# A masked attention and MLP kernel on Trainium2: the second MLP product of chunks 4 to 11 in seven block products per pair

## The chip, the cores and the metric

The kernel runs on one core of one Trainium2 chip. The metric is the device time of one execution in microseconds (us); three runs of the kernel before gave a median of 678.27 us (676.78 to 681.28). The engines are TensorE (PE; its weight loads are listed apart as PEld), VectorE (DVE), ScalarE (ACT), GpSimd (POOL) and SyncE (SP, which here only issues DMA transfers).

## The reference, cut to what matters

```python
# attention: batch 4, 8 heads, 768 positions, 64 per head, float32
scores = q @ k.T / sqrt(64)      # kept where key < 4 (sinks) or 0 <= query - key < 128
x = softmax(scores) @ v          # brought to 3072 tokens x 512
# MLP
h = x @ w_in                                            # 512 -> 2048
g = np.maximum(h, 0.0) + alpha * np.minimum(h, 0.0)     # alpha: one per column of h
out = g @ w_out                                         # 2048 -> 512
```

## The kernel before

**Tiling.** The 3072 tokens are cut into 12 chunks (`NCHUNK`) of 256 (`QC`), three per batch. The 2048 columns of h are 16 blocks (`NF`) of 128, called f. For a chunk c and a block f, GEMM1 (`gemm1`, L887) computes a transposed block of h, 128 x 256, in a PSUM bank, and GEMM2 (`gemm2`, L906) adds the product of that block of g with 128 rows of w_out to two PSUM banks of 128 tokens x 512, which hold the sums over all 16 f. The work on PE is done in a 32-bit form (`F32R`) that holds fewer bits of the mantissa; each operand is split into a high and a low part, and a product is three matmuls: high x high, high x low, low x high. So GEMM1 has 4 x 3 = 12 matmuls of 256 columns per (c, f) (L894), and GEMM2 has 2 x 3 = 6 of 512 columns (L931, L932 and L929).

**From GEMM1 to GEMM2.** ACT scales the PSUM bank by alpha (L898), DVE takes the maximum of the bank and that (L899), which is g; ACT casts g to its high part gh (L900), DVE subtracts for the low part gl (L901). gh and gl have three buffers each, g two. When a chunk is complete, ACT copies both banks (L937) and SP issues two output transfers of 256 KB (L938). For the last f of the last chunk, lines L912 to L923 do this bank by bank, with the transfers issued from ACT.

**Attention of the next chunk** is woven into GEMM1 and GEMM2 of the present one. Per head: SP loads q and k (`stage`, L443), ACT casts (L561, L562) and DVE subtracts (L563 for k, L565 for q) to make the parts, PE makes scores for two halves u (L597, L598), DVE masks and takes the minimum (L610), ACT takes the exponential (L614), DVE scales (L655), GpSimd makes the small sink products (L659). For every pair of heads DVE transposes blocks of 32 (L741), SP sends them through a DRAM scratch and back (L744, L746), and DVE applies triangle masks (L757, L759, L770). At the end `av_four` (L848) multiplies by v on PE (L786, L859, L875), and ACT and DVE write the high and the low part of x, `xh` and `xl` (L881, L882), which have two buffers, so that one chunk's x can be written while another's is read.

**Weights** are loaded and converted once, in chunks 0 and 1, into 16 resident tiles `fin` (high and low parts of both matrices).

**The order of work** is written out by a planner. Every piece of work is an `op` with an engine, a cost and the values that it reads and writes; `draw` (L153) plays all engines forward by these costs and picks, at each step, the operation that can start first, with ties within 0.1 to 0.2 us broken by rank. A PE operation's rank is its place in the program; any other has the rank of the first operation that needs it, or of its own place plus 12 (`LATEST`). Some operations name a second engine (`other`), and the planner takes the one that starts first, with 0.3 us against the second. The result is a fixed order for each engine; SP's DMA issues are ordered by it too. An `op` can be marked `locks`: the planner then lets no two marked operations on DVE and GpSimd overlap. In the kernel before nothing is marked. The loop at L1065 lays out (c, f) in order, GEMM2 two blocks behind GEMM1 (`LAG`).

**PSUM** has eight banks: two for scores (`s`), two for attention products (`pa`), two for h, two for the output sums (`o`).

## Time and profile before

| | us |
|---|---|
| median of three runs | 678.27 (676.78 to 681.28) |
| profiled execution, first to last instruction (its span; the time around it is not recorded) | 676.2 |
| PE busy | 663.8 |
| DVE busy | 525.8 |
| ACT busy | 397.5 |
| GpSimd busy | 34.5 |
| output copies of chunks 2, 3, 10 and 11 (start) | 209.43, 262.23, 628.72, 669.94 |

A period between two output copies holds one chunk's GEMM1 and GEMM2 and the attention of the next. DMA moves 85.19 MB at a mean of 126 GB/s over the span. In the timeline, "0.39 PE L931 MATMUL" is an instruction of 0.39 us of line 931; matmuls overlap, so their pace is the distance of their starts. An arrow in brackets names what ended the idle time before an instruction. In a group's row the numbers after the bar are the busy time of the group, the mean ns of one and the idle time of the engine in front of them.

### The profile page before, as it was taken

The page shows a single profiled execution, that of the slowest core. Times are in us where ns is not written, and L with a number is a line of the kernel's source. Part 1 is how long each engine was busy: PE and PEld are TensorE (multiplying, and loading weights), DVE is VectorE, ACT ScalarE, POOL GpSimd, SP SyncE. Part 2 cuts the span into 40 slices and gives each one's busy share as a digit, 9 for nine tenths or more (in the row PEclk, how much of TensorE's full clock was granted, in tenths as well). Part 3 has the DMA queues.
Part 4 walks back from the last instruction along what each step waited for, and adds up shares of the span by engine and source line. Part 5 has one row for each costly group of instructions (what it writes and reads, how often), then busy time and mean ns, then how long its engine had stood idle before and what let it go on. Part 6 is the DMA issues. An engine that isn't in the chain of part 4 may idle for free.

```text
span 676.2 us, 13243 instructions
## 1 busy us (share of the span) xinstructions
PE 663.8 (98%) x4532; PEld 580.5 (86%) x4534; DVE 525.8 (78%) x1750; ACT 397.5 (59%) x1066; POOL 34.5 (5%) x115
## 2 busy tenths in 40 slices
...
GB/s 314 229 277 151 241 187 39 127 71 147 122 133 107 122 148 93 145 132 95 141 118 114 143 107 93 163 140 61 172 128 78 161 128 88 142 94 17 32 2 35
DMA packets 58683, 85.19 MB, mean 126 GB/s; under 512 B 9072, under 2 KB 35056, under 8 KB 58608
## 3 DMA queue, kind: packets, MB, share of 16 engines
...
q8 instruction: 37, 0.61, 0.4%
...
## 4 chain that ended last, share of the span: by engine, by line
PE 83%; DVE 9%; ACT 5%; issue 2%; POOL 0%; DMA 0%; ACTq 0%; SPq 0%; POOLq 0%
PE bank L894 35%; PE bank L931 12%; PE bank L932 11%; PE bank L929 11%; PE bank L786 3%; PE bank L598 3%; PE bank L597 3%; PE bank L875 2%; DVE wa L396 2%; ACT pt L614 1%; ACT wa L382 1%; DVE wa L394 1%; DVE w L404 1%; DVE g L899 1%; DVE gl L901 1%
## 5 line engine op out<-in xcount | busy, mean ns | idle before, releaser
L894 PE MATMUL bank<-xh,w 128*128 128x256 f32 x1536 | 307.9, 283 | 0.4 <-DVE g L899 0.2
L894 PEld LDWEIGHTS bank<-xh,w 128*128 128x128 f32 x1536 | 250.6, 189 | 9.0 <-DVE g L899 3.0
L894 PE MATMUL bank<-xl,w 128*128 128x256 f32 x768 | 215.1, 280 | 0.1
L898 ACT ACTIVATE g<-bank,param 128x256 f32<-128x256 f32 x192 | 90.5, 472 | 117.4 <-PE bank L894 113.1
L931 PE MATMUL bank<-w,gh 128*128 128x512 f32 x382 | 151.7, 397 | 0.2 <-ACT gh L900 0.2
L932 PE MATMUL bank<-w,gh 128*128 128x512 f32 x382 | 150.1, 393 | 0.0
L894 PEld LDWEIGHTS bank<-xl,w 128*128 128x128 f32 x768 | 145.2, 189 | 4.4 <-DVE xl L808 0.3
L614 ACT ACTIVATE pt<-pt,nm 128x260 f32<-128x260 f32 (+1 forms) x192 | 94.5, 493 | 53.5 <-DVE nm L610 53.1
L899 DVE TENSOR_TENSOR g<-bank,g 128x256 f32<-128x256 f32 x192 | 79.7, 419 | 51.4 <-ACT g L898 50.9
L929 PE MATMUL bank<-w,gl 128*128 128x512 f32 x382 | 119.5, 394 | 0.0
L900 ACT CAST gh<-g 128x256 fp32r<-128x256 f32 x192 | 76.9, 404 | 59.7 <-DVE g L899 59.6
L901 DVE TENSOR_TENSOR gl<-g,gh 128x256 fp32r<-128x256 f32 x192 | 80.5, 423 | 26.5 <-ACT gh L900 23.0
L610 DVE CUSTOM_DVE_ANT_0 pt<-bank,masks 128x260 f32<-128x260 f32 (+1 forms) x192 | 75.0, 401 | 19.3 <-PE bank L598 15.5
L929 PEld LDWEIGHTS bank<-w,gl 128*128 128x128 f32 x382 | 70.7, 188 | 16.2 <-issue 0.7
L931 PEld LDWEIGHTS bank<-w,gh 128*128 128x128 f32 x382 | 71.9, 188 | 9.5 <-ACT gh L900 0.7
L932 PEld LDWEIGHTS bank<-w,gh 128*128 128x128 f32 x382 | 71.9, 188 | 8.3
L563 DVE TENSOR_TENSOR kq<-stage,kq 64x392 fp32r<-64x392 f32 x80 | 45.3, 566 | 2.7
L659 POOL TENSOR_TENSOR sink<-pt,ri 128x8 f32<-128x8 f32 x80 | 20.8, 264 | 504.7 <-DVE ri L644 358.8
L597 PE MATMUL bank<-kq 128*128 128x260 f32 (+1 forms) x160 | 44.4, 278 | 1.3 <-DVE nm L610 1.3
L598 PE MATMUL bank<-kq 128*128 128x260 f32 (+1 forms) x160 | 45.0, 281 | 0.0
L655 DVE CUSTOM_DVE_ANT_0 comb<-pt,ri 128x128 f32<-128x128 f32 x136 | 43.1, 343 | 0.4
L561 ACT CAST kq<-stage 128x392 fp32r<-128x392 f32 x80 | 40.9, 512 | 0.7 <-ACT pt L614 0.2
...
## 6 DMA issues: line engine op xcount, KB each, us to landing
...
swap<-comb SPq DMA_DIRECT2D x36, 256.0 KB, 2.0
comb<-swap SPq DMA_DIRECT2D x36, 256.0 KB, 3.2
...
out_dram<-ob SPq DMA_DIRECT2D x22, 256.0 KB, 3.5
...
```

What stands on the lines that cost most here:

```text
L597: nc.tensor.matmul(s[:, w0], qh()[:, qs], ks()[:, kw], start=True, stop=False)
L598: nc.tensor.matmul(s[:, w0], ql()[:, qs], ks()[:, kw], start=False, stop=True)
L610: op("DVE", dve(n), lambda: nc.vector.tensor_tensor_reduce(out=pt.at[:, u, w0], in0=s.at[:, w0], in1=masks[:, i, w0], scale=-0.125, scalar ...
L614: op("ACT", exp(n), lambda: nc.scalar.activation(pt.at[:, u, w0], pt.at[:, u, w0], AF.Exp, bias=nm.at[:, h, u:u + 1], scale=-1.0, accum_ou ...
L894: nc.tensor.matmul(h(), fin.at[:, 0, part, ks], rhs.at[:, kt], start=(kt == 0 and n == 0), stop=(kt == KT - 1 and n == 2))
L898: op("ACT", act(QC, True), lambda: nc.scalar.activation(g.at, h(), AF.Copy, scale=alt[:, f:f + 1]), reads=[bk, known("param")], writes=[g])
L899: op("DVE", dve(QC), lambda: nc.vector.tensor_tensor(g.at, h(), g.at, ALU.max), reads=[bk], writes=[g])
L900: op("ACT", cast(QC), lambda: nc.scalar.copy(gh.at, g.at), reads=[g], writes=[gh])
L901: op("DVE", dve(QC), lambda: nc.vector.tensor_tensor(gl.at, g.at, gh.at.bitcast(F32), ALU.subtract), reads=[g, gh], writes=[gl])
L929: nc.tensor.matmul(o2[j].at, gl.at[:, js], fin.at[:, 1, 0], start=False, stop=(f == NF - 1))
L931: nc.tensor.matmul(o2[j].at, gh.at[:, js], fin.at[:, 1, 0], start=(f == 0), stop=False)
L932: nc.tensor.matmul(o2[j].at, gh.at[:, js], fin.at[:, 1, 1], start=False, stop=False)
```

## The change

From chunk 4 (`SECOND`) on, GEMM2 takes two f blocks at a time. Their two 128 x 256 blocks of g and the two 128 x 512 row blocks of w_out are seen as 2 x 2 blocks (g in blocks of 128 tokens, w_out in halves of 256 columns, `HALF`), and the product is made with seven block products instead of eight (`seven`), each of three matmuls of 256 columns. For it:

- `blocks` makes the sums of g blocks: per pair one sum of 256 and two of 128 elements, on GpSimd or, where the planner finds that earlier, on DVE. The high and low parts are made of 2 + 2 + 3 blocks of 128 instead of 4, in new tiles ta, tb and ha (two buffers), hb and hc (one).
- `prepare` makes the combined weights in chunk 2, per pair p with eight GpSimd operations and two ACT casts, and writes them to a DRAM scratch `tees`. `exchange` loads one combined block over half a resident weight tile; the three others are loaded again for each chunk and pair, in three transfers of 256 KB into four buffers `st`. These are the former second buffers of xh and xl, which have one from chunk 4 on.
- The products go into four PSUM banks (`o` twice, `z`, `y`) and are combined at the end of a chunk by one ACT copy and five DVE operations, then sent out in two transfers (from ACT in the last chunk).
- The four banks s and pa become z, y, one bank `s2` for scores and one `pa2`; `av_four` uses pa2 and s2.
- From the attention of chunk 5 on, q's low part goes to GpSimd, or to DVE where that is earlier. These, the sums, the new low parts and `prepare` are marked `locks`.
- The attention of the next chunk is spread over 13 of 16 blocks (`SOON`) with `av_four` at the last, and some operations get earlier due times (`DUE`). GEMM2 of a pair comes one pair behind its GEMM1. `after_all` makes the new uses of a shared tile wait for all former users.

The diff, cut to its core:

```diff
+SECOND = 4
+SOON = 13
+DUE = {'bank': 4, 'scores': 5, 'swap': 8, None: 14}
+HALF = DM // 2
...
+    both = pool.tile([P, 4, HALF], F32, name="both")
+    plan.kind("ob", [both[:, 2 * i:2 * i + 2].rearrange("p b x -> p (b x)") for i in range(2)])
+    plan.kind("ob2", [both])
+    xs = {n: [pool.tile([P, KT, QC], F32R, name=f"{n}{i}") for i in range(2)] for n in ("xh", "xl")}
+    for n in xs:
+        plan.kind(n, xs[n])
+        plan.kind(n + "2", xs[n][:1])
+    plan.kind("st", [xs[n][1][:, 2 * i:2 * i + 2] for n in xs for i in range(2)])
+    exact = pool.tile([P, 16 * P], F32, name="exact")
+    cut = pool.tile([P, 18 * P], F32R, name="cut")
+    plan.kind("g", [exact[:, i * P:(i + 2) * P] for i in (12, 14)])
+    plan.kind("gh", [cut[:, i * P:(i + 2) * P] for i in (6, 8, 10)])
+    plan.kind("gl", [cut[:, i * P:(i + 2) * P] for i in (12, 14, 16)])
+    plan.kind("prep", [exact[:, :12 * P]])
+    some_blocks = lambda t, a, n: t[:, a * P:(a + n) * P].rearrange("p (b x) -> p b x", x=P)
+    plan.kind("ta", [some_blocks(exact, i, 3) for i in (0, 13)])
+    plan.kind("tb", [some_blocks(exact, i, 5) for i in (3, 8)])
+    plan.kind("ha", [some_blocks(cut, i, 4) for i in (0, 4)])
+    plan.kind("hb", [some_blocks(cut, 8, 4)])
+    plan.kind("hc", [some_blocks(cut, 12, 6)])
+    for name, i in (("s2", 0), ("z", 1), ("pa2", 2), ("y", 3)):
+        plan.kind(name, [banks[i]])
+    tees = [held(scratch.tile([P, 4, 2, HALF], F32, name=f"tee{i}")) for i in range(NF // 2)]
...
-           reads=[st, (kq, "q")], writes=[(kq, "l")])
+        low = lambda on: on.tensor_tensor(ql(), q_raw(), qh().bitcast(F32), ALU.subtract)
+        if c > SECOND:
+            op("POOL", pool2(QC), lambda: low(nc.gpsimd), reads=[st, (kq, "q")], writes=[(kq, "l")], locks=True,
+               other=("DVE", dve(QC), lambda: low(nc.vector)))
+        else:
+            op("DVE", dve(QC), lambda: low(nc.vector), reads=[st, (kq, "q")], writes=[(kq, "l")])
         prep[c, h] = (kq, qh, ql, ks)
 
...
         else:
             pair = (h,)
-            banks_ = [val("s")]
+            banks_ = [val("s2" if c > SECOND else "s")]
+            if c == SECOND + 1 and h == u == 0:
+                late.append((banks_[0], ("s", "pa")))
...
     def begin_x(c, p):
         if p == 0:
-            xh[c], xl[c] = val("xh"), val("xl")
+            xh[c], xl[c] = (val("xh2"), val("xl2")) if c >= SECOND else (val("xh"), val("xl"))
+            if c == SECOND:
...
         def some(kt):
@@ -894,6 +937,8 @@
                 nc.tensor.matmul(h(), fin.at[:, 0, part, ks], rhs.at[:, kt], start=(kt == 0 and n == 0), stop=(kt == KT - 1 and n == 2))
         for kt in range(KT):
             op("PE", 3 * mm(QC), lambda kt=kt: some(kt), reads=[fin, (x1, kt), (x2, kt)], writes=[bk], tail=R_TAIL)
+        if c >= SECOND:
+            return blocks(c, f, bk)
         g, gh, gl = val("g"), val("gh"), val("gl")
         op("ACT", act(QC, True), lambda: nc.scalar.activation(g.at, h(), AF.Copy, scale=alt[:, f:f + 1]), reads=[bk, known("param")], writes=[g])
+    def blocks(c, f, bk):
+
+        if f % 2 == 0:
+            twos[c, f // 2] = [val(n) for n in ("ta", "tb", "ha", "hb", "hc")]
+        ta, tb, ha, hb, hc = five = twos[c, f // 2]
+        h = lambda: bk.at[:, :QC].rearrange("p (b x) -> p b x", x=P)
+
+        def either(cost, cost2, run, reads, writes):
+            op("POOL", cost, lambda: run(nc.gpsimd), reads=reads, writes=writes, locks=True, other=("DVE", cost2, lambda: run(nc.vector)))
+
+        def cast_part(to, t, a, n):
+            op("ACT", cast(n * P), lambda: nc.scalar.copy(to.at[:, :n], t.at[:, a:a + n]), reads=[(t, i) for i in range(a, a + n)], writes=[(to, 0)])
+
+        def low_part(to, t, a, n):
+            op("DVE", dve(n * P), lambda: nc.vector.tensor_tensor(to.at[:, n:], t.at[:, a:a + n], to.at[:, :n].bitcast(F32), ALU.subtract),
+               reads=[(to, 0)] + [(t, i) for i in range(a, a + n)], writes=[(to, 1)], locks=True)
+        t, steps_ = ((ta, slice(0, 3, 2)), (tb, slice(3, 5)))[f % 2]
+        place, keys = lambda: t.at[:, steps_], [(t, i) for i in range(5)[steps_]]
+        op("ACT", act(QC, True), lambda: nc.scalar.activation(place(), h(), AF.Copy, scale=alt[:, f:f + 1]), reads=[bk, known("param")], writes=keys).due = "bank"
+        op("DVE", dve(QC), lambda: nc.vector.tensor_tensor(place(), h(), place(), ALU.max), reads=[bk], writes=keys).due = "bank"
+        if f % 2 == 0:
+            either(pool2(P), dve(P), lambda on: on.tensor_tensor(ta.at[:, 1], ta.at[:, 2], ta.at[:, 0], ALU.subtract), [(ta, 0), (ta, 2)], [(ta, 1)])
+            cast_part(ha, ta, 0, 2)
+            low_part(ha, ta, 0, 2)
+            return
+        either(pool2(QC), dve(QC), lambda on: on.tensor_tensor(tb.at[:, 1:3], tb.at[:, 4:5].broadcast_to([P, 2, P]), ta.at[:, 1:3], ALU.add),
+               [(tb, 4), (ta, 1), (ta, 2)], [(tb, 1), (tb, 2)])
+        cast_part(hb, tb, 3, 2)
+        either(pool2(P), dve(P), lambda on: on.tensor_tensor(tb.at[:, 0], tb.at[:, 3], tb.at[:, 1], ALU.subtract), [(tb, 3), (tb, 1)], [(tb, 0)])
+        low_part(hb, tb, 3, 2)
+        cast_part(hc, tb, 0, 3)
+        low_part(hc, tb, 0, 3)
...
+    def prepare(p):
+
+        v, tee = val("prep"), tees[p]
+        t = lambda a, b: v.at[:, a * HALF:b * HALF].rearrange("p (b x) -> p b x", x=HALF)
+        flat = lambda i: v.at[:, i * DM:(i + 1) * DM]
+        for j in range(2):
+            fin = fins[2 * p + j]
+            op("POOL", pool2(DM), lambda fin=fin, j=j: nc.gpsimd.tensor_tensor(
+                flat(j), fin.at[:, 1, 0].bitcast(F32), fin.at[:, 1, 1].bitcast(F32), ALU.add), reads=[fin], writes=[(v, 2 * j), (v, 2 * j + 1)], locks=True)
+        for to, a, b in ((0, 1, 0), (1, 1, 3), (3, 3, 0), (2, 2, 3)):
+            op("POOL", pool2(HALF), lambda to=to, a=a, b=b: nc.gpsimd.tensor_tensor(t(to, to + 1), t(a, a + 1), t(b, b + 1), ALU.subtract),
+               reads=[(v, a), (v, b)], writes=[(v, to)], locks=True)
+        for j in range(2):
+            keys = [(v, 2 * j), (v, 2 * j + 1)]
+            op("ACT", cast(DM), lambda j=j: nc.scalar.copy(flat(2).bitcast(F32R), flat(j)), reads=keys, writes=[(v, 4)])
+            op("POOL", pool2(DM), lambda j=j: nc.gpsimd.tensor_tensor(flat(j), flat(j), flat(2), ALU.subtract), reads=[(v, 4)], writes=keys, locks=True)
+            for i, b in ((0, 4), (1, 2 * j)):
+                op("SP", ISSUE, lambda i=i, b=b, j=j: nc.sync.dma_start(tee.at[:, 2 * j:2 * j + 2, i], t(b, b + 2)),
+                   reads=[(v, b), (v, b + 1)], writes=[(tee, (i, j))], nbytes=4 * P * DM)
+
+    def exchange(p):
+        fin, tee = fins[2 * p], tees[p]
+        op("SP", ISSUE, lambda: nc.sync.dma_start(fin.at[:, 1, :, HALF:].bitcast(F32), tee.at[:, 0]),
+           reads=[tee], writes=[(fin, "t")], nbytes=8 * P * HALF)
+
+    def seven(c, p, dst):
+
+        (ta, tb, ha, hb, hc), one, two = twos.pop((c, p)), fins[2 * p], fins[2 * p + 1]
+        if p == 0:
+            acc[c] = [val("o"), val("o"), val("z"), val("y")]
+            if c == SECOND:
+                late.extend((x, ("s", "pa",)) for x in acc[c][2:])
+        x, y, z, w_ = acc[c]
+        lent_ = {}
+        for b in (1, 2, 3):
+            st = lent_[b] = val("st")
+            op("SP", ISSUE, lambda st=st, b=b: nc.sync.dma_start(st.at.bitcast(F32), tees[p].at[:, b]),
+               reads=[tees[p]], writes=[st], nbytes=8 * P * HALF)
+            if c == SECOND and p < 2:
+                late.append((st, ("xh", "xl",)))
+        fixed = lambda fin, j: (fin, lambda i: fin.at[:, 1, i, j * HALF:(j + 1) * HALF])
+        moved = lambda b: (lent_[b], lambda i: lent_[b].at[:, i])
+        parts = [(ha, 0, fixed(one, 0), z, 0, True), (ha, 1, moved(1), w_, 1, True), (hb, 0, fixed(two, 0), x, 0, True), (hb, 1, moved(2), y, 0, True),
+                 (hc, 1, moved(3), z, 1, False), (hc, 2, fixed(one, 1), w_, 0, False), (hc, 0, fixed(two, 1), x, 1, False)]
+        if (c, p) == (NCHUNK - 1, NF // 2 - 1):
+            parts = [parts[i] for i in (0, 1, 4, 5, 2, 3, 6)]
+        for t, blk, (src, rhs), bank_, half, first in parts:
+            def some(t=t, blk=blk, rhs=rhs, bank_=bank_, half=half, first=first, last=not first or bank_ is y):
+                to, n = bank_.at[:, half * HALF:(half + 1) * HALF], 3 if t is hc else 2
+                nc.tensor.matmul(to, t.at[:, blk], rhs(0), start=first and p == 0, stop=False)
+                nc.tensor.matmul(to, t.at[:, blk], rhs(1), start=False, stop=False)
+                nc.tensor.matmul(to, t.at[:, n + blk], rhs(0), start=False, stop=last and p == NF // 2 - 1)
+            op("PE", 3 * mm(HALF), some, reads=[src, t], writes=[bank_], tail=R_TAIL)
+        if p < NF // 2 - 1:
+            return
+        o = val("ob2")
+        if c == SECOND:
+            late.append((o, ("ob",)))
+        view = lambda b: b.at.rearrange("p (b x) -> p b x", x=HALF)
+        k = lambda *n: [(o, i) for i in n]
+        op("ACT", cast(DM, True), lambda: nc.scalar.copy(o.at[:, 0:4:3], view(z)), reads=[z], writes=k(0, 3))
+        op("DVE", dve(HALF), lambda: nc.vector.tensor_tensor(o.at[:, 3], o.at[:, 3], o.at[:, 0], ALU.add), reads=k(0), writes=k(3))
+        op("DVE", dve(DM), lambda: nc.vector.tensor_tensor(o.at[:, 1:3], view(w_), o.at[:, 3:4].broadcast_to([P, 2, HALF]), ALU.add),
+           reads=[w_] + k(3), writes=k(1, 2))
+        op("DVE", dve(HALF), lambda: nc.vector.tensor_tensor(o.at[:, 3], w_.at[:, :HALF], o.at[:, 2], ALU.add), reads=[w_] + k(2), writes=k(3))
+        op("DVE", dve(DM), lambda: nc.vector.tensor_tensor(o.at[:, 0:2], view(x), o.at[:, 0:2], ALU.add), reads=[x], writes=k(0, 1))
+        op("DVE", dve(HALF), lambda: nc.vector.tensor_tensor(o.at[:, 2], y.at[:, :HALF], o.at[:, 2], ALU.add), reads=[y], writes=k(2))
+        for j in range(2):
+            engine, on, cost = ("ACT", nc.scalar, 0.1) if c == NCHUNK - 1 else ("SP", nc.sync, ISSUE)
+            op(engine, cost, lambda j=j, on=on: on.dma_start(dst(j), o.at[:, 2 * j:2 * j + 2].rearrange("p b x -> p (b x)")),
+               reads=k(2 * j, 2 * j + 1), nbytes=4 * P * DM)
+        del acc[c]
...
+            gemm2(*pend[0], dst(pend[0][0]))
+            if pend[0][0] == SECOND - 1 and pend[0][1] % 2:
+                exchange(pend[0][1] // 2)
+            pend.pop(0)
         for st in todo[cut:]:
...
+        if c == SECOND - 2 and f % 2:
+            prepare(f // 2)
+    left = [lambda a=a: (gemm2(*a, dst(a[0])), exchange(a[1] // 2) if a[1] % 2 else None) for a in pend]
+    plan.bound = plan.rank
+    for c in range(SECOND, NCHUNK):
+        todo = stretched(c + 1)
+        for f in range(NF):
+            if (c, f) == (NCHUNK - 1, NF // 2):
+                judge()
+            gemm1(c, f)
+            cut = round(len(todo[f]) / 2) if f % 2 else len(todo[f])
+            for st in todo[f][:cut]:
+                st()
+            if len(left) > 1 or f % 2:
+                left.pop(0)()
+            for st in todo[f][cut:]:
+                st()
+            if f % 2:
+                left.append(lambda c=c, f=f: seven(c, f // 2, dst(c)))
+    for st in left:
+        st()
...
```

74 lines of the change are left out of this document (38 added, 36 removed).

## The prediction

> **What bounds the kernel now.** I read the page first, then busy time by stretches, then the order of time on TensorE (PE), then the groups of one chunk's stretch.
>
> ```profile
> span 676.2 us, 13243 instructions
> PE 663.8 (98%) x4532; PEld 580.5 (86%) x4534; DVE 525.8 (78%) x1750; ACT 397.5 (59%) x1066; POOL 34.5 (5%) x115
> PE 83%; DVE 9%; ACT 5%; issue 2%; POOL 0%; DMA 0%; ACTq 0%; SPq 0%; POOLq 0%
> ```
>
> PE is busy 98% of the span and 83% of the chain that ended last. Busy time says little where matmuls overlap, so I look at the stretch in which GEMM2 changes: from the output copy of chunk 3 to that of chunk 10 (columns: length, then busy us of PE, PEld, DVE, ACT, POOL, granted clock, DMA share, GB/s).
>
> ```profile
> 262.23:628.72 366.49, 366.31 (x2567) 329.63 (x2566) 291.04 (x1056) 203.35 (x583) 16.54 (x58) 1.00 0.40 118
> ```
>
> These are seven periods (chunks 4 to 10), 52.36 us each, with PE never idle and its clock at 1.00. Per chunk DVE is busy 291.04 / 7 = 41.6 us, ACT 29.1, GpSimd (POOL) 2.4. So PE sets the pace and DVE stands 20% below it. The order of time shows what a matmul costs:
>
> ```profile
> 400.71 0.28 PE L894 MATMUL bank<-xh,w 128*128 128x256 f32 x1
> ...
> 402.09 0.39 PE L931 MATMUL bank<-w,gh 128*128 128x512 f32 x1
> ...
> 403.47 0.28 PE L894 MATMUL bank<-xh,w 128*128 128x256 f32 x1
> ```
>
> From 400.71 to 402.09 run twelve GEMM1 matmuls of 256 columns: 1.38 us, 0.115 each. From 402.09 to 403.47 run six GEMM2 matmuls of 512: 1.38 us, 0.23 each. The 0.28 and 0.39 are latencies that overlap. Both pay by the column; a weight load for every 256 columns costs nothing extra.
>
> **The change, part by part.**
>
> *Matmuls.* Two f blocks of GEMM2 take 12 matmuls of 512 columns now, 2.76 us. Seven products of three matmuls at 256 columns are 21 x 0.115 = 2.415 us. That saves 0.345 us a pair, 2.76 us a chunk, and over 8 pairs x 8 chunks **22.1 us**. PE's period becomes 52.36 - 2.76 = 49.6 us. There are 72 more weight loads a chunk, at GEMM1's proven pace.
>
> *VectorE and ScalarE.* One period's rows, in the stretch from 366.63 to 419.40:
>
> ```profile
> L901 DVE TENSOR_TENSOR gl<-g,gh 128x256 fp32r<-128x256 f32 x16 | 6.7, 424 | 1.8 <-ACT gh L900 1.4
> L655 DVE CUSTOM_DVE_ANT_0 comb<-pt,ri 128x128 f32<-128x128 f32 x16 | 4.9, 342 | 0.1
> L563 DVE TENSOR_TENSOR kq<-stage,kq 64x392 fp32r<-64x392 f32 x8 | 4.5, 564 | 0.2
> L561 ACT CAST kq<-stage 128x392 fp32r<-128x392 f32 x8 | 4.1, 511 | 0.0
> L565 DVE TENSOR_TENSOR kq<-stage,kq 128x256 fp32r<-128x256 f32 x9 | 3.8, 422 | 0.2
> L770 DVE TENSOR_TENSOR wa<-comb,tri 128x256 f32<-128x256 f32 x8 | 3.0, 406 | 0.0
> L759 DVE TENSOR_TENSOR comb<-comb,tri 128x256 f32<-128x256 f32 x4 | 1.5, 421 | 0.0
> L757 DVE TENSOR_TENSOR comb<-comb,tri 128x256 f32<-128x256 f32 x4 | 1.5, 420 | 0.0
> L882 DVE TENSOR_TENSOR xl<-bank,xh 128x512 fp32r<-128x512 f32 x2 | 1.4, 692 | 3.7 <-ACT xh L881 3.7
> L690 DVE TENSOR_TENSOR ts<-sink,ts 128x128 fp32r<-128x128 f32 x1 | 0.3, 293 | 0.0
> ```
> ```profile
> 399.89 0.76 DVE L759 TENSOR_TENSOR comb<-comb,tri 128x256 f32<-128x256 f32 x2
> ```
>
> Two instructions of 0.42 end after 0.76: the next starts 0.08 before the last has ended. So one in a row occupies DVE for its duration less 0.08: 0.21 us at 128 elements (L690), 0.34 at 256, 0.61 at 512 (L882), and 0.475 at 384, by interpolation. Per pair, a new low part of 384 elements comes (hc): 8 x 0.475 = +3.8 us a chunk. The final combination of the four banks is three operations of 256 and two of 512: 1.02 + 1.22 = +2.2. The low part of q (L565) goes to GpSimd: 8 x 0.34 = -2.7. DVE: 41.6 + 3.8 + 2.2 - 2.7 = **44.9 us** of 49.6, if all sums of g blocks run on GpSimd. If DVE did these sums (two of 128, one of 256 a pair: 0.76, 6.1 a chunk) and q's low part as well, it would need 44.9 + 6.1 + 2.7 = 53.7, more than PE. ACT gets one cast of 384 a pair (L561's 0.511 for 392): 8 x 0.5 = 4, 33 of 49.6 us; it stays hidden, below DVE.
>
> *GpSimd.* Its nearest rows, 64x512 and 128x8, are far apart (minimum/median/maximum):
>
> ```profile
> L467 POOL TENSOR_TENSOR vs<-ob,vs x3: 1282/1286/1507, 155.3 to 454.4; 64x512 fp32r<-64x512 f32 x3
> L659 POOL TENSOR_TENSOR sink<-pt,ri x80: 199/236/1256, 113.2 to 603.0; 128x8 f32<-128x8 f32 x80
> ```
>
> (1.282 - 0.199) / 504 = 2.15 ns an element: 0.46 us at 128, 0.73 at 256. A pair's sums take 2 x 0.46 + 0.73 = 1.65, a head's low q part 0.73: 8 x 2.38 = 19.0 us a chunk. GpSimd has time for that. The maximum of 1256 points to the real cost. Two places in the order of time:
>
> ```profile
> 297.15 1.56 DVE L565 TENSOR_TENSOR kq<-stage,kq 128x256 fp32r<-128x256 f32 x1
> ```
> ```profile
> 297.15 1.28 POOL L467 TENSOR_TENSOR vs<-ob,vs 64x512 fp32r<-64x512 f32 x1 [8.52 <-issue]
> ```
> ```profile
> 155.51 0.43 DVE L808 TENSOR_TENSOR xl<-bank,xh 128x256 fp32r<-128x256 f32 x1 [0.53 <-ACT xh L805]
> 155.85 0.42 DVE L610 CUSTOM_DVE_ANT_0 pt<-bank,masks 128x260 f32<-128x260 f32 x1
> ```
> ```profile
> 155.34 1.29 POOL L467 TENSOR_TENSOR vs<-ob,vs 64x512 fp32r<-64x512 f32 x1 [0.58 <-POOL sink L659]
> ```
>
> At 297.15 a DVE operation with both inputs in SBUF, normally 0.42, starts with GpSimd's 1.28 and takes 1.56: it stood still until GpSimd was done. At 155.5, under the same GpSimd operation, two that read a PSUM bank run at full speed. So GpSimd's time is taken from DVE wherever DVE has two SBUF inputs next. Bounds: nothing (GpSimd runs only beside PSUM readers and idle time) to all 19.0 us a chunk. The planner keeps the new sums and low parts of g out of each other's way (`locks`); it doesn't know of L655, L563, L770, L757 and L759, 15.4 us of 52.8, a share of 0.29. I take 0.29 x 19.0 = 5.5: DVE 44.9 + 5.5 = **50.4 us**, 0.8 above PE's 49.6. That makes DVE the pace, weakly: 7 x 0.8 = **+5.6 us**.
>
> The Trainium skill says more (Perfetto Trace Analysis, Optimizing Scalar/DVE Operations): since GpSimd and DVE share a port, moving work between them might not help. By that the sums would cost as on DVE; this is the second rival below.
>
> *Making the combined weights.* Per pair four GpSimd operations of 512 and four of 256: 4 x 1.28 + 4 x 0.73 = 8.0 us, 64 us for eight pairs, beside the periods of chunks 2 and 3:
>
> ```profile
> 157.18:209.43 52.25, 51.65 (x355) 46.62 (x356) 39.83 (x139) 27.96 (x82) 2.08 (x7) 1.00 0.37 111
> 209.43:262.23 52.80, 52.80 (x375) 47.53 (x374) 42.10 (x156) 29.42 (x85) 2.05 (x8) 1.00 0.41 121
> ```
>
> DVE has 12.4 and 10.7 us free in them, 23 in all. Blocking by the share of all two-input rows (with L901 and L565 25.9 of 52.8, 0.49) is 31 us, in pieces of up to 1.28; the small sink products (L659) wait in GpSimd's queue. The free time hides most of it, and chunk 4 can take a rest: I take **+2**, with bounds 0 and 8 (31 - 23). Its two ACT casts of 512 and four DMA issues a pair lie beside ACT's 24 free us and SP's idle time.
>
> *Streaming.* Each pair reads three blocks of 256 KB, 6.3 MB a chunk.
>
> ```profile
> q1 hardware_dynamic: 5376, 6.33, 41.1%
> ```
> ```profile
> comb<-swap SPq DMA_DIRECT2D x4, 256.0 KB, 3.3
> ```
> ```profile
> SPq L443 <- DVE gl L901: 15.2, 3, 9.8
> SPq L443 <- DVE kq L565: 8.2, 4, 4.3
> ```
>
> Twice the bytes in the same stretch is 41.1% x 2 x 52.8 / 49.6 = 88% of the engines at today's packets: high, not full. Four buffers serve three blocks, so the last block's buffer comes free one pair (6.2 us) before its next use; a 256 KB read lands in 3.3. That hides it with 2.9 to spare; on the path I put 0. What is queued behind: SP works in order, and a stage load that waits for its buffer (in this period three waits of 15.2 in all for one releaser, four of up to 4.3 for another) holds the blocks issued after it. Such waits now mostly show that SP has nothing else to do. A block load that waits for PE likewise holds the stage, v and swap transfers.
>
> *Single x and single score bank.* xh and xl lose their second buffer: copies for the next chunk wait for the last GEMM1. They take about 0.6 (ACT) + 0.7 (DVE, L882) until the first half is there. The pair left over (2.4 us on PE) covers them: 0; without it 1.3 x 7 = 9 us. Scores share one bank with spread-out due times: 0. hb and hc have one buffer: hc's cast waits until the pair before is multiplied, and its 0.5 (ACT) and 0.56 (DVE) must end before the next pair's last three products, two GEMM1 (2.76) later: 0, with some 3 us for DVE's queue; where DVE is later than that, the port term above counts it.
>
> *End.*
>
> ```profile
> 670.21 0.39 PE L918 MATMUL bank<-w,gl 128*128 128x512 f32 x1
> ```
> ```profile
> 671.02 0.58 ACT L921 COPY ob<-bank 128x512 f32<-128x512 f32 x1 [0.49 <-PE bank L918]
> 671.64 0.36 ACTq L922 DMA_DIRECT2D out_dram<-ob  x1
> ```
>
> Now one ACT copy of 0.58 lies between the last matmul and the last output. Afterwards there are a DVE operation of 512 and one of 256, 0.61 + 0.42 = 1.03, and the last pair's longer chain of sums has little PE work over it: **+1.0**, bounds 0 and 3.
>
> *Sum*, in the profiled execution's own span: 676.2 - 22.1 + 5.6 + 2 + 1.0 = 662.7. The median of the runs shown, 678.27, is 2.1 above that span, so I forecast **664.8 us**, 2.0% less. A measurement of this kernel tells about 1% (6.8 us) from no change.
>
> **Rivals.**
>
> 1. *PE stays the only bound.* If at most (49.6 - 44.9) / 19.0 = 0.25 of GpSimd's time blocks DVE, each period is 49.6 and the prepare stage hides: 676.2 - 22.1 + 1.0 = 655.1, **657 us** as a median. For: PE now has no gap in 366 us, and the sums can choose DVE where it is free. Against: 0.25 is less than the share I count.
>
> 2. *The port: the sums cost as much as on DVE.* Place: chunks 4 to 10, DVE's two-input operations behind GpSimd's. Price: DVE 53.7 us a period, 1.3 more than today. It is 676.2 + 7 x 1.3 - 2.8 (chunk 11, no attention) + 3 = 685.5, **688 us**. It decides from a blocked share of 0.39 on, where 44.9 + 7.4 reaches today's 52.36; 53.7 is 0.46. For: 297.15 shows the whole 1.28 lost, and with L901 and L565 the share is 0.49. Against: those are just what the plan keeps apart.
>
> 3. *The stream comes late.* A stage load's wait of 4.3 us (the shorter kind) ahead of a block exceeds the 2.9 of slack, once a chunk, and loaded DMA engines add the like of 0.4: 1.8 a chunk, 8 x 1.8 = 14.4. Without the port's 5.6 that is 676.2 - 22.1 + 14.4 + 3 = 671.5, **674 us**. For: 88% DMA load and one in-order queue. Against: SP's order comes from the same plan, which would put the block first.
>
> **How the numbers follow.** Forecast 0.38, rival 1 0.22, rival 2 0.20, rival 3 0.20. Faster by over 1% (under 671.5): the forecast and rival 1, 0.60. Of rivals 2 and 3, rival 3 falls within 1% and rival 2 mostly beyond it (0.18): within 1% 0.22. The forecast's own range, from a blocked share of 0.25 to 0.39 and the small bounds, is 657 to 675. To hold 8 of 10 the range reaches past rival 1 below and to rival 2 above: 655 to 688.
>
> **What would show it.** Right: 21 GEMM2 matmuls a pair at 0.115; periods near 50.4 us; DVE over 90% busy there, with its two-input rows' means well above 0.42 and PE's small gaps ended by DVE low parts; GpSimd near 19 us a period; DMA shares near 0.8. Rival 1: periods of 49.6 with PE without gaps. Rival 2: periods above 52.4 and DVE full. Rival 3: PE waiting for DMA into the streamed tiles. The forecast is wrong if the sum of periods 4 to 10 isn't near 353 us, or if chunks 2 and 3 grow by more than 10.

## The result and the profile after

The changed kernel takes **753.73 us** (median of 4 runs, 751.1 to 760.69), the kernel before 679.14 (4 runs, 676.78 to 681.28): a ratio of 1.112, with a 95% interval of 1.1062 to 1.1178. The forecast was 664.8 with a range of 655 to 688, so it was wrong in sign and the range missed. The profiled execution took 754.88 us, its span is 752.8. That is 76.6 us more than the span before.

The page of the changed kernel: span, busy time by engine, the chain that ended last, the main DMA queue (packets, MB, share of 16 engines).

```profile
span 752.8 us, 15401 instructions
PE 676.4 (90%) x5110; PEld 607.8 (81%) x5110; DVE 629.3 (84%) x1799; ACT 430.4 (57%) x1137; POOL 275.4 (37%) x427
PE 35%; DVE 31%; DMA 10%; issue 3%; ACT 2%; POOL 1%; SPq 0%; DVEq 0%; POOLq 0%; ACTq 0%
q1 hardware_dynamic: 93584, 132.00, 57.5%
```

PE's share of the chain fell from 83% to 35%; DVE (31%) and DMA (10%), 9% and 0% before, are on the path. To place the 76.6 us, here is busy time by stretches of the changed kernel, cut at the output copies of chunks 2, 3 and 10 (columns as in the prediction):

```profile
0.00:237.12 237.12, 210.34 (x1334) 167.23 (x1335) 212.09 (x511) 157.59 (x385) 92.07 (x113) 0.97 0.56 181
237.12:292.61 55.49, 55.27 (x394) 50.00 (x393) 43.80 (x159) 31.91 (x91) 6.79 (x16) 1.00 0.59 172
292.61:699.57 406.96, 367.56 (x3022) 347.76 (x3021) 350.58 (x1080) 222.51 (x623) 162.16 (x275) 0.98 0.71 213
699.57:752.80 53.23, 43.25 (x367) 42.81 (x365) 22.81 (x52) 18.39 (x42) 14.39 (x24) 0.96 0.43 135
```

Before, the same stretches took 209.43, 52.80, 366.49 and 47.48 us. So chunks 0 to 2 lost 27.7, chunk 3 lost 2.7, chunks 4 to 10 lost 40.5 where the forecast had a gain of 13.7, and the end lost 5.75. Chunk 4's output copy falls early in its period, since the products lag less there (its stretch holds 150 matmuls of GEMM1, a later period 192). I therefore compare six periods, from the copy of chunk 4 to that of chunk 10, in every kernel; first before, then after:

```profile
315.44:629.19 313.75, 313.57 (x2195) 282.18 (x2195) 247.93 (x901) 173.46 (x496) 13.31 (x49) 1.00 0.40 116
```
```profile
345.20:699.57 354.37, 320.05 (x2634) 303.10 (x2633) 305.86 (x939) 193.94 (x543) 140.66 (x239) 0.98 0.70 212
```

The period went from 52.3 to 59.1 us. DVE is busy 305.86 / 6 = 51.0 us of it, almost what the prediction gave as its need (50.4). What the prediction did not have is the rest: for 8.1 us of every period DVE, whose load is now above the 49.6 us that PE needs, stands before an operation that it cannot start yet. The six are not alike: 56.4, 60.5, 63.9, 57.8, 58.3 and 57.5 us, with a granted clock of 0.97 in the second, 0.92 in the third and 1.00 in the others.

The groups of one period of the changed kernel (busy us, mean ns) show the shared port at work:

```profile
L976 POOL TENSOR_TENSOR exact<-exact 128x256 f32<-128x256 f32 x8 | 6.9, 863 | 2.3 <-DVE exact L970 1.5 <-DVE nm L648 0.4
L648 DVE CUSTOM_DVE_ANT_0 pt<-bank,masks 128x260 f32<-128x260 f32 x16 | 6.8, 423 | 0.3
L693 DVE CUSTOM_DVE_ANT_0 comb<-pt,ri 128x128 f32<-128x128 f32 x16 | 6.7, 451 | 0.2
L965 DVE TENSOR_TENSOR cut<-exact,cut 128x256 fp32r<-128x256 f32 x16 | 6.4, 409 | 0.0
L595 DVE TENSOR_TENSOR kq<-stage,kq 64x392 fp32r<-64x392 f32 x8 | 5.4, 670 | 0.2
L808 DVE TENSOR_TENSOR wa<-comb,tri 128x256 f32<-128x256 f32 x8 | 4.4, 593 | 0.0
```

L693, L595 and L808 are the prediction's L655, L563 and L770, the ones the planner doesn't hold apart: 342, 564 and 406 ns have become 451, 670 and 593, 4.1 us in this period. The mask on the score bank (L648, reads PSUM) and the low parts under `locks` (L965) keep their 0.42 and 0.41. It is GpSimd and not the stream that slows the three: over six periods they take 349, 564 and 420 ns in the kernel below that has all sums on DVE and streams as much, and 440, 696 and 476 in the one without a stream.

Where DVE stands idle, the view of its waits in the six periods says (us in total, times, longest), first before, then after:

```profile
DVE g L899 <- ACT g L898: 22.0, 24, 1.5
DVE xl L882 <- ACT xh L881: 17.1, 12, 3.1
```
```profile
DVE xl L925 <- ACT xh L924: 21.3, 12, 6.1
DVE comb L795 <- DMA comb<-swap: 7.8, 6, 2.1
DVE both L1052 <- ACT both L1051: 7.7, 6, 1.3
```

All three of the changed kernel stand at a chunk's end: the copies of x for the next chunk, the swapped rows of the last heads, the final combination. They are 36.8 of the 48.5 us. The order of time shows one such end (TensorE, then DVE; the time in brackets is idle time before, and its releaser):

```profile
454.15 0.97 PE L902 MATMUL bank<-sinkT,vs 128*128 128x256 f32 x4 [2.07 <-DMA sinkT<-turns]
455.05 3.33 PE L824 MATMUL bank<-wa,v 128*64 128x256 f32 x24
458.21 1.90 PE L918 MATMUL bank<-comb,v 128*64 128x256 f32 x24
```
```profile
453.95 1.22 DVE L965 TENSOR_TENSOR cut<-exact,cut 128x256 fp32r<-128x256 f32 x3
459.05 0.69 DVE L925 TENSOR_TENSOR xl<-bank,xh 128x512 fp32r<-128x512 f32 x1 [3.89 <-ACT xh L924]
```

DVE is done with all that it has at 455.17. TensorE waits for the transposed sinks, then multiplies the attention matrix, and only then come ACT's copy and DVE's. DVE gets no other work meanwhile, because GEMM1 of the next chunk needs those very copies. This end is one of two (in the second and third period) at which the granted clock fell: it was 0.62 from 454 to 456 and 0.53 from 456 to 458. The same 24 matmuls of L824 took 3.33 and 3.68 us in these two, but 1.96 at a clock of 1.00, as in the fifth period:

```profile
635.69 0.74 PE L902 MATMUL bank<-sinkT,vs 128*128 128x256 f32 x4 [1.52 <-DMA sinkT<-turns]
636.36 1.96 PE L824 MATMUL bank<-wa,v 128*64 128x256 f32 x24
```

So over 1 us of the 3.89 shown is the clock's.

### The profile page after: what moved, and what is told of

It is laid out like the page before. It is cut to its first block, busy times and chain, and to the rows that moved or that the text cites. A ratio compares the mean times of both kernels' runs of the same rounds, so it can differ in the third digit from the quotient of the medians.

```text
span 752.8 us, 15401 instructions
## 1 busy us (share of the span) xinstructions
PE 676.4 (90%) x5110; PEld 607.8 (81%) x5110; DVE 629.3 (84%) x1799; ACT 430.4 (57%) x1137; POOL 275.4 (37%) x427
## 3 DMA queue, kind: packets, MB, share of 16 engines
q1 hardware_dynamic: 93584, 132.00, 57.5%
## 4 chain that ended last, share of the span: by engine, by line
PE 35%; DVE 31%; DMA 10%; issue 3%; ACT 2%; POOL 1%; SPq 0%; DVEq 0%; POOLq 0%; ACTq 0%
PE bank L937 12%; DVE pt L648 4%; DVE kq L595 4%; DVE comb L693 4%; DVE cut L965 4%; DVE wa L808 3%; DMA sinkT<-turns 3%; PE bank L1040 3%; PE bank L824 3%; PE bank L1042 3%; PE bank L1041 3%; DMA turns<-pt 3%; DVE exact L970 2%; PE bank L918 2%; PE bank L1079 2%
## 5 line engine op out<-in xcount | busy, mean ns | idle before, releaser
L937 PEld LDWEIGHTS bank<-xh,w 128*128 128x128 f32 x1536 | 249.8, 190 | 13.5 <-DVE exact L944 7.1
L962 ACT CAST cut<-exact 128x256 fp32r<-128x256 f32 (+1 forms) x192 | 80.5, 437 | 65.9 <-POOL exact L979 35.3
L972 POOL TENSOR_TENSOR exact<-exact 128x128 f32<-128x128 f32 x64 | 33.6, 525 | 189.0 <-DVE exact L970 165.6
L965 DVE TENSOR_TENSOR cut<-exact,cut 128x256 fp32r<-128x256 f32 (+1 forms) x192 | 89.5, 490 | 12.3 <-ACT cut L962 9.5
L969 ACT ACTIVATE exact<-bank,param 128x256 f32<-128x256 f32 x128 | 60.3, 471 | 53.2 <-PE bank L937 52.7
L648 DVE CUSTOM_DVE_ANT_0 pt<-bank,masks 128x260 f32<-128x260 f32 (+1 forms) x192 | 75.6, 400 | 14.6 <-PE bank L636 10.1
L635 PE MATMUL bank<-kq 128*128 128x260 f32 (+1 forms) x160 | 50.7, 317 | 30.9 <-DVE nm L648 29.9
L1040 PE MATMUL bank<-w,cut 128*128 128x256 f32 x256 | 73.1, 285 | 0.0
L1042 PE MATMUL bank<-w,cut 128*128 128x256 f32 x256 | 72.2, 282 | 0.6 <-DVE cut L965 0.6
L1041 PE MATMUL bank<-w,cut 128*128 128x256 f32 x256 | 71.7, 280 | 0.0
L976 POOL TENSOR_TENSOR exact<-exact 128x256 f32<-128x256 f32 x64 | 53.9, 842 | 34.1 <-DVE exact L970 30.0
L970 DVE TENSOR_TENSOR exact<-bank,exact 128x256 f32<-128x256 f32 x128 | 52.0, 417 | 10.3 <-ACT exact L969 10.0
L595 DVE TENSOR_TENSOR kq<-stage,kq 64x392 fp32r<-64x392 f32 x80 | 56.6, 707 | 2.6
L693 DVE CUSTOM_DVE_ANT_0 comb<-pt,ri 128x128 f32<-128x128 f32 x136 | 55.0, 429 | 1.0
L597 POOL TENSOR_TENSOR kq<-stage,kq 128x256 fp32r<-128x256 f32 x56 | 47.1, 842 | 22.6 <-ACT kq L594 22.6
L1079 PE MATMUL bank<-w,cut 128*128 128x512 f32 x128 | 51.4, 402 | 0.5 <-ACT cut L945 0.5
```

What stands on the lines that cost most here:

```text
L595: op("DVE", dve(KC), lambda: nc.vector.tensor_tensor(ks()[D:], k_raw()[D:], ks()[D:].bitcast(F32), ALU.subtract), reads=[st], writes=[(kq, ...
L635: nc.tensor.matmul(s[:, w0], qh()[:, qs], ks()[:, kw], start=True, stop=False)
L648: op("DVE", dve(n), lambda: nc.vector.tensor_tensor_reduce(out=pt.at[:, u, w0], in0=s.at[:, w0], in1=masks[:, i, w0], scale=-0.125, scalar ...
L693: op("DVE", 0.28, lambda u=u, jk=jk: nc.vector.tensor_tensor_reduce(out=view()[:, u], in0=pt.at[:, u, 0:P], in1=pt.at[:, u, P + NS:], scal ...
L937: nc.tensor.matmul(h(), fin.at[:, 0, part, ks], rhs.at[:, kt], start=(kt == 0 and n == 0), stop=(kt == KT - 1 and n == 2))
L962: op("ACT", cast(n * P), lambda: nc.scalar.copy(to.at[:, :n], t.at[:, a:a + n]), reads=[(t, i) for i in range(a, a + n)], writes=[(to, 0)])
```

## The experiments

Each kernel was measured once with a profile, beside the kernel before on the same chip (676.36 to 676.78 us). Each result gives the total and the row of its own six periods; "DVE idle" is (length minus DVE busy) / 6. Since the changed kernel's own four runs lie between 751.1 and 760.69, a few us in a total say little; and with every edit the planner draws a new order, which can cost or save time by itself.

**Undoing one part each.** First, the combined weights: GpSimd's sums begin behind GEMM1 of chunk 2, pair by pair, where the code places them.

```diff
-    def prepare(p):
+    def prepare(p, since):
...
+            plan.order_after(sum_, since)
```

> The making of the combined weights may start only once GEMM1 of chunk 2 has reached the pair (in the changed kernel it began at 28.7 us, in chunk 0, because GpSimd was free and nothing held it back). Theory A (GpSimd's time is taken from DVE by the shared port, and in chunks 0 to 2 DVE is full): the copy of chunk 2 comes near 215 us instead of 237, with some of the cost moved to chunks 3 and 4, so 735 to 742 us in all against 755. Rival (the amount of work, not its place, costs the time): the same 25 us come back in chunks 2 to 4, and the total stays at 750 to 757.

753.14 us in all. Chunk 2 is copied at 226.09 instead of 237.12 and chunk 3 at 274.25 instead of 292.61, but chunk 4 pays it back (stretch of chunk 4, then the six periods):

```profile
274.25:346.72 72.47, 58.84 (x439) 54.76 (x440) 53.38 (x155) 35.26 (x95) 32.58 (x50) 0.84 0.65 198
346.72:698.92 352.20, 316.91 (x2634) 300.82 (x2633) 305.58 (x939) 193.60 (x543) 140.40 (x239) 0.99 0.70 213
```

Chunk 4 took 72.5 us there against 52.6, so at its copy the two kernels are level (346.72 against 345.20). The price of the weights did not vanish by waiting. The granted clock in chunk 4 was 0.84; how much of its 19.9 us is the clock's, this run does not separate.

Second, two banks for scores, as before:

```diff
-    for name, i in (("s2", 0), ("z", 1), ("pa2", 2), ("y", 3)):
-        plan.kind(name, [banks[i]])
+    for name, which in (("s2", (0, 2)), ("z", (1,)), ("y", (3,))):
+        plan.kind(name, [banks[i] for i in which])
...
```

> The scores of chunks 5 on use two PSUM banks in turn (the one that only the attention products held is shared). Theory B (one score bank ties PE to DVE: PE stood 22 us in chunks 4 to 10 for the mask operation that reads the bank): the mean period of chunks 4 to 10 falls from 58.1 to about 55, total about 732 us. Theory A alone (DVE's throughput behind the port sets the end): PE waits for the same DVE a little later, periods 57.5 to 58.5, total 750 to 757.

748.08 us, close to the unchanged total; a period of 57.3:

```profile
345.56:689.10 343.54, 313.94 (x2579) 297.03 (x2578) 302.33 (x938) 191.21 (x543) 140.43 (x239) 0.99 0.71 217
```

Third, no sums of g blocks: the products read the blocks themselves, so the output's chunks 4 to 11 leave out the algorithm's sums.

```diff
+        made = lambda t, a, n: t.at[:, 0:3:2] if t is ta else t.at[:, 3:5] if n == 2 else t.at[:, 3:4].broadcast_to([P, 3, P])
...
-            either(pool2(P), dve(P), lambda on: on.tensor_tensor(ta.at[:, 1], ta.at[:, 2], ta.at[:, 0], ALU.subtract), [(ta, 0), (ta, 2)], [(ta, 1)])
...
-        either(pool2(QC), dve(QC), lambda on: on.tensor_tensor(tb.at[:, 1:3], tb.at[:, 4:5].broadcast_to([P, 2, P]), ta.at[:, 1:3], ALU.add),
...
-        either(pool2(P), dve(P), lambda on: on.tensor_tensor(tb.at[:, 0], tb.at[:, 3], tb.at[:, 1], ALU.subtract), [(tb, 3), (tb, 1)], [(tb, 0)])
```

> Leaves out the three sums of g blocks of each pair (the casts and low parts read blocks that exist), so the products are not the right ones; all else stays, with q's low part still on GpSimd. It takes about 14 of 23 us of GpSimd's time a period away and the sums' place in the chain from GEMM1 to the products. Theory A: DVE's lost time of 7.6 us a period more than halves and the period falls to 51 to 53, total 705 to 718. Theory B or the stream: periods stay above 55.5, total above 735.

726.52 us, between the two expectations; a period of 54.7, DVE busy 46.7:

```profile
343.86:672.29 328.43, 311.10 (x2634) 298.17 (x2633) 280.04 (x940) 195.26 (x544) 51.23 (x95) 1.00 0.74 228
```

Fourth, no stream: the products read the resident weight blocks in place of the combined ones, and none of these is loaded again for each chunk and pair.

```diff
-        for b in (1, 2, 3):
-            st = lent_[b] = val("st")
-            op("SP", ISSUE, lambda st=st, b=b: nc.sync.dma_start(st.at.bitcast(F32), tees[p].at[:, b]),
...
-        moved = lambda b: (lent_[b], lambda i: lent_[b].at[:, i])
+        moved = lambda b: fixed((one, one, two, two)[b], b % 2)
```

> Leaves out the 192 reloads of combined weights from DRAM in chunks 4 to 11 (the products use resident halves, so the output is not the right one); making and storing them stays. Theory C (the stream delays the other transfers on SP's queue: PE stood 12 us for the sink transfer and more in DVE's waits for the swaps): periods fall from 58.1 to 55 or less, total under 735. Theory A: under 1 us a period, total 748 to 757.

732.68 us; a period of 55.9. DVE is as busy as in the changed kernel, 51.3, but idle only 4.65 instead of 8.1:

```profile
343.85:679.43 335.58, 313.57 (x2634) 297.26 (x2633) 307.68 (x939) 193.83 (x543) 141.72 (x239) 0.99 0.36 109
```

**The products alone.** The third and fourth edits together, no weights prepared, and the low part of q back on DVE. It leaves out the combined weights and the sums. What is left of the change is 21 matmuls of 256 columns where twelve of 512 stood, the low part of hc, the final combination, the single banks and buffers, and the new spread of the attention.

```diff
-        if c > SECOND:
+        if c > NCHUNK:
...
-        if c == SECOND - 2 and f % 2:
-            prepare(f // 2)
```

> Leaves out the combined weights (made, stored, exchanged and streamed) and the sums of g blocks, and q's low part is back on DVE: what stays is the seven products, the new low parts, the banks and the combination at the end. The output is not the right one. If the prediction's PE term holds (0.345 us a pair), the periods of chunks 4 to 10 are 49.6 to 50.5, chunk 2's copy comes at 209 to 213 us, and the total is 655 to 664. If the new banks or the single x cost time by themselves, periods stay above 51.5 and the total above 670.

674.83 us; chunk 2 is copied at 208.74 and the period is 52.2:

```profile
308.88:622.12 313.24, 305.46 (x2634) 294.45 (x2633) 285.39 (x985) 195.84 (x543) 13.97 (x49) 1.00 0.39 119
```

This is the study's plainest result. PE's need fell by 2.76 us a period and the period stayed where it was (52.3). Chunks 0 to 3 end within 2 us of before, so the 27.7 us lost by chunk 2's copy belong to the combined weights.

**Port, or the sums' own work?** The third edit's reads, but the sums are still computed and not used (ACT's cast reads in the same way):

```diff
-            op("DVE", dve(n * P), lambda: nc.vector.tensor_tensor(to.at[:, n:], t.at[:, a:a + n], to.at[:, :n].bitcast(F32), ALU.subtract),
+            op("DVE", dve(n * P), lambda: nc.vector.tensor_tensor(to.at[:, n:], made(t, a, n), to.at[:, :n].bitcast(F32), ALU.subtract),
```

> The sums of g blocks are made as in the changed kernel, on GpSimd, but nothing reads them: the casts and low parts read the blocks of the run without sums, so the output is not the right one. Theory A (the port): the period stays at 56.5 to 58, total 742 to 755, although the sums are no longer in the chain from GEMM1 to the products. Theory D (the sums' latency in that chain is the cost): the period is that of the run without sums, 53.7, total about 727.

748.42 us, a period of 58.4:

```profile
343.54:694.08 350.54, 318.37 (x2634) 300.61 (x2633) 309.80 (x940) 194.16 (x545) 139.93 (x240) 0.99 0.69 213
```

No operation reads these sums any more, and still they cost 3.7 us a period against the kernel without them. DVE is busy 5.0 us longer for (139.93 - 51.23) / 6 = 14.8 us of GpSimd, with the same DVE instructions: a blocked share of 0.34. That is GpSimd's work beside DVE's, not the latency of the sums.

All sums and q's low part on DVE:

```diff
-            op("POOL", cost, lambda: run(nc.gpsimd), reads=reads, writes=writes, locks=True, other=("DVE", cost2, lambda: run(nc.vector)))
+            op("DVE", cost2, lambda: run(nc.vector), reads=reads, writes=writes)
...
```

> All sums of g blocks and q's low parts on DVE; GpSimd keeps only the small sink products and, before chunk 4, the combined weights. By the rows of before DVE then needs 53.7 us a period. Theory A (GpSimd's help costs DVE about as much as it takes off): periods 56 to 59, total 742 to 760. If GpSimd's help is worth its 8.8 us of DVE time: periods of 62 or more, total above 780.

770.51 us, between the two expectations; a period of 61.3 with DVE busy 54.8:

```profile
347.54:715.59 368.05, 328.09 (x2634) 304.69 (x2633) 329.01 (x1129) 199.38 (x544) 14.29 (x49) 0.99 0.66 204
```

So GpSimd does help, by 2.3 us a period. And the planner told of the port for the five groups that it did not know (L655, L563, L770, L757 and L759 of the kernel before):

```diff
-            reads=[st], writes=[(kq, "k")])
+            reads=[st], writes=[(kq, "k")], locks=True)
...
-                reads=[(pt, u), ri], writes=[(cb, (h % 2, u)), jk])
+                reads=[(pt, u), ri], writes=[(cb, (h % 2, u)), jk], locks=True)
...
```

> The planner is told of the port for the attention's two-input DVE operations too (the ones of k, the scaling and the triangle masks are marked locks); the work is the same. If the loss is that the plan doesn't know of them (the 0.29 share of the prediction), DVE's lost time of 7.6 us a period falls below 4 and periods fall to 54 to 56, total 725 to 740. If the port has no free time to give, the wait is only moved: periods 57 to 60, total 747 to 770.

747.69 us, a period of 57.9:

```profile
345.43:693.07 347.64, 317.80 (x2634) 300.61 (x2633) 302.58 (x940) 193.39 (x543) 137.14 (x239) 0.99 0.70 215
```

DVE is busy 0.5 us less. Holding operations apart in the plan recovers little: over six periods L808 falls from 594 to 472 ns, but the low parts of 256 (L965) grow from 427 to 495.

**Why do the products alone gain nothing?** Two score banks for the kernel of products alone, then also two buffers for the copies of x:

```diff
-    for name, i in (("s2", 0), ("z", 1), ("pa2", 2), ("y", 3)):
+    for name, which in (("s2", (0, 2)), ("z", (1,)), ("y", (3,))):
...
```

> The run with the products only (sums, combined weights and stream left out, so not the right output), with two score banks in turn. From the copy of chunk 4 to that of chunk 10 the run with one bank took 313.2 us, as long as the kernel before (313.8), with gaps of 17.8 us on PE, 12 of them around the scores. Theory B (the single bank ties PE to DVE, which is 90% busy): gaps fall to 6 or less, the stretch to 300 to 303, the total to 660 to 663. Theory A' (DVE at 90% is late whatever the banks): gaps stay above 12, the total above 668.

```diff
-        plan.kind(n + "2", xs[n][:1])
+        plan.kind(n + "2", xs[n])
...
```

> As the run before it, and x has its second buffer back (free since nothing is streamed). If the single x costs time too, the stretch falls by another 2 to 5 us; if the left-over pair covers its copies, as the prediction had it, by less than 1.5.

683.65 and 681.9 us, periods of 53.2 and 53.3: neither buffer is the cause. That a bank more made the kernel 8.8 us slower shows what a newly drawn order can do.

```profile
311.39:630.70 319.31, 308.02 (x2634) 294.66 (x2633) 286.81 (x985) 194.93 (x543) 14.33 (x49) 1.00 0.38 116
```
```profile
309.39:628.93 319.54, 308.50 (x2634) 295.18 (x2633) 286.97 (x985) 194.99 (x544) 14.38 (x49) 1.00 0.38 116
```

TensorE's waits of the products alone, then of the kernel with two score banks, show that the wait for DVE only moves, from the scores' bank to GEMM1's:

```profile
PE bank L635 <- DVE nm L648: 5.2, 10, 0.7
```
```profile
PE bank L937 <- DVE exact L972: 10.5, 16, 0.9
```

If DVE itself is the cause, less DVE work must speed this kernel up. It leaves out hc's low part, and those products read the high part twice:

```diff
-        low_part(hc, tb, 0, 3)
...
-                to, n = bank_.at[:, half * HALF:(half + 1) * HALF], 3 if t is hc else 2
+                to, n = bank_.at[:, half * HALF:(half + 1) * HALF], 0 if t is hc else 2
```

> The run with the products only, and the low part of hc (3.8 us of DVE a period) is left out too; its products read the high part instead, so PE's work is the same (not the right output). Theory E (DVE's busy time plus what it must stand at a chunk's end is the period): from the copy of chunk 4 to that of chunk 10 the 313.2 us fall by 12 to 20, to 293 to 301 (49.6 to 50.2 a period where PE takes over), total 655 to 662. If another part of the seven products sets the period: 309 or more, total 668 or more.

665.05 us, 3 us above the lower expectation and as much below the other. With DVE at 43.8 the period is 50.6, with PE busy 99% of it: 1.7 of the seven products' 2.76 us appear as soon as DVE has room.

```profile
308.77:612.55 303.78, 301.75 (x2634) 293.49 (x2633) 262.85 (x937) 194.62 (x543) 13.68 (x49) 1.00 0.40 121
```

And the reverse: the kernel before, with DVE work added whose result nothing uses (one or two operations of 256 for each f block of chunks 4 to 11).

```diff
...
+        for _ in range(1 + f % 2 if c >= 4 else 0):
+            jg = val("jg")
+            op("DVE", dve(QC), lambda jg=jg: nc.vector.tensor_tensor(jg.at, g.at, gh.at.bitcast(F32), ALU.subtract), reads=[g, gh], writes=[jg])
```

> The kernel before, correct, with 24 more DVE operations of 256 elements in each of chunks 4 to 11 that nothing reads (8.1 us, DVE at 49.7 of 52.3 a period, as loaded as in the changed kernel), and no GpSimd, stream or product changed. Theory E: DVE becomes the pace, periods of 53.5 to 55, total 685 to 697. If DVE at 95% still hides behind PE, as the prediction's step took it: 52.3 to 52.8 and 676 to 681.

707.74 us, above both expectations; DVE busy 49.4, the period 56.5:

```profile
316.47:655.56 339.09, 323.93 (x2198) 288.23 (x2197) 296.14 (x1050) 175.48 (x499) 13.10 (x49) 0.97 0.36 108
```

49.4 us of DVE would fit into the 52.3 us period if DVE could be nearly full. It was not: 7.2 us a period stay idle, and the kernel before becomes 31 us slower without a product, a stream or a sum changed. Where the 7.2 lie was only read: the view of DVE's waits has 17.3 us in the six periods for the scores (L611) and less for all else. These are five waits of 3.0 to 3.9 us, each ending 1.5 us before an output copy, while TensorE multiplies the attention matrix. Part of that is the fixed order and not a dependency: at 427.55 DVE starts L611, which it had waited for, and only then the low part of x, whose input ACT had begun to copy at 424.92 in 0.59 us. Two things stay open in this run. The granted clock was 0.97 against 1.00 before, which can make up at most 0.03 x 339 = 10 of the 25 us that the six periods gained (an estimate from these figures). And the added operations also hold the buffers of g and gh longer.

**Where does the stream cost?** Streaming only for the first five of a chunk's eight pairs (the last three read resident blocks):

```diff
-        for b in (1, 2, 3):
+        for b in (1, 2, 3) if p < 5 else ():
...
```

> The changed kernel without the reloads of pairs 5, 6 and 7 of each chunk (their products read resident halves, so not the right output); pairs 0 to 4 are streamed. No stream at all gained 3.2 us a period. If the stream's cost sits in the sink and swap transfers at a chunk's end, most of that comes back: periods 2.2 to 3.5 shorter, total 728 to 738. If it is spread over the chunk, three eighths: 1.2 a period, total 744 to 749.

732.27 us, a period of 56.3, DVE idle 4.9; the row, and DVE's wait for the copies of x:

```profile
341.09:679.02 337.93, 311.98 (x2634) 296.48 (x2633) 308.75 (x940) 193.64 (x543) 141.98 (x238) 1.00 0.58 179
```
```profile
DVE xl L925 <- ACT xh L924: 5.4, 8, 1.0
```

With five eighths of the stream kept, nearly all of its cost is gone (732.68 without any). So nearly all of it comes from the loads for the last three pairs of each chunk. Issuing the stream from ScalarE's queue instead of SP's:

```diff
-            op("SP", ISSUE, lambda st=st, b=b: nc.sync.dma_start(st.at.bitcast(F32), tees[p].at[:, b]),
+            op("ACT", 0.12, lambda st=st, b=b: nc.scalar.dma_start(st.at.bitcast(F32), tees[p].at[:, b]),
```

> The changed kernel, correct, with the 192 reloads issued from ACT's queue instead of SP's. Theory C1 (SP's in-order queue holds the swap, sink and stage transfers behind reloads that wait for PE): the 12.3 us of PE's waits for the sink transfer shrink below 4, total 735 to 745. Theory C2 (the transfers themselves slow each other on the DMA engines: swaps land in 3.1 instead of 2.0 us): total 750 to 758.

764.43 us, a period of 59.8: above both expectations, and no gain. It with the two score banks and the wider `locks`, which had each come out some 6 us lower alone:

> Correct; two score banks, all two-input DVE operations marked locks, and the reloads issued from ACT. If the three gains add up (7, 7 and up to 10 us): 730 to 738 us. If they are the same loss seen three times: 742 to 748. In either case slower than before.

769.98 us, again above both expectations; a period of 60.9:

```profile
349.58:714.97 365.39, 326.42 (x2634) 306.87 (x2633) 305.87 (x940) 190.68 (x543) 140.41 (x239) 0.97 0.65 203
```

Its waits for the transposed sinks grew to 15.4 us in six periods (5.4 in the kernel with ScalarE's queue alone, 10.0 in the changed kernel). Why these two lose is read from waits and was not taken apart further. None of the variants of the changed kernel that compute everything beats the kernel before; the fastest is the one with more `locks`, 747.69 us.

## Why the prediction was wrong

Its sum against the spans. The measured terms come from the stretches above, with 2.76 us a chunk kept as the matmuls' own; the period's term is 406.96 - (366.49 - 7 x 2.76), the end's 53.23 - (47.48 - 2.76).

| term | forecast | measured |
|---|---|---|
| fewer matmul columns | -22.1 | -22.1 |
| chunks 4 to 10, above PE's need | +5.6 | +59.8 |
| making the weights (chunks 0 to 3) | +2 | +30.4 |
| the end | +1.0 | +8.5 |
| sum | -13.5 | +76.6 |

The cuts also move GEMM1 between the rows. As the traces count them, the stretch of chunk 3 has 212 matmuls of GEMM1 instead of 195, chunks 4 to 10 have 1302 instead of 1349, the end 192 instead of 168. At 0.115 us each, some 2.0 us of chunk 3's 2.7 and 2.8 us of the end's 8.5 are work taken from chunks 4 to 10, whose own loss is some 5 us larger than its row.

**Matmuls: right.** With DVE out of the way (products with less DVE work) 19 steps between products' matmuls take 2.16 us, 0.114 each (399.79 to 401.95), and PE's period is 50.6 us, against 49.6. The price holds; it is no longer the price that sets the time.

**VectorE's load: right.** 51.0 us busy against 50.4. Without GpSimd and with q on DVE it was 47.6, and 47.6 - 2.7 = 44.9 is the prediction's figure before the port. The blocked share was 0.34 for the sums against 0.29, on a little more GpSimd time: 127.35 / 6 = 21.2 us a period above before, against 19.0, at 863 ns an operation of 256 instead of 730. All on DVE: 54.8 measured, 53.7 predicted. For the whole, (51.0 - 44.9) / 21.2 is again 0.29. That this share came out is in part luck: it was argued from the groups that the planner doesn't hold apart, and with all of them held apart DVE was busy only 0.5 us less.

**The step that failed** is the one that made time out of loads: "DVE 44.9 + 5.5 = 50.4 us, 0.8 above PE's 49.6. That makes DVE the pace, weakly: 7 x 0.8 = +5.6 us." It takes the larger of two engines' needs as the period, as if that engine could be busy all the time. The runs show that the idle part beside DVE's busy time is never small, and changes from kernel to kernel:

| kernel | DVE busy | DVE idle | period |
|---|---|---|---|
| before | 41.3 | 11.0 | 52.3 (PE full) |
| products, less DVE work | 43.8 | 6.8 | 50.6 (PE 99%) |
| products alone | 47.6 | 4.6 | 52.2 |
| no stream | 51.3 | 4.65 | 55.9 |
| stream not at the end | 51.5 | 4.9 | 56.3 |
| no sums | 46.7 | 8.1 | 54.7 |
| all locks | 50.4 | 7.5 | 57.9 |
| changed kernel | 51.0 | 8.1 | 59.1 |
| sums on DVE | 54.8 | 6.5 | 61.3 |
| before, more DVE work | 49.4 | 7.2 | 56.5 |

In the runs that the table leaves out it is 5.4 to 9.9 us. So DVE was idle at least 4.6 us a period, for the most part in the chain at a chunk's end (attention product, ACT's copy of x, DVE's low part) and in hops between engines. The products alone are the plainest case: DVE's 47.6 us are less than PE's 49.6, and the period was 52.2. The stream adds some 3. The measured 59.1 divides into 50.4 + 0.6 (load) + 4.65 (idle part without a stream) + 3.4 (the rest, the stream's); this is a division of the measured period and no test of it. The rows that the prediction quotes had the sign of it: L882 waits 3.7 us a period for ACT although PE was never idle. The prediction used only that row's duration. At a load of 50 us such a wait is on the path. That a new order could fill part of it was not tried. By this reading the products' 2.76 us were lost before any port or stream: the added low parts and combinations on DVE (3.8 + 2.2) outweigh them.

**Rival 2** (the port, slower) had the side and a true mechanism, and too small a price for the same reason: 53.7 us was again a load taken as a period. The Trainium skill's rule (Perfetto Trace Analysis, Optimizing Scalar/DVE Operations) that moving work between GpSimd and DVE might not help fell the other way here: on DVE the sums and q's low part cost 2.3 us a period more. The Trainium skill's page SBUF — State Buffer (SBUF: two separate sides) says that of a DVE operation with two SBUF inputs and a GpSimd operation that reads SBUF, the one that starts first holds the shared port and the other is blocked until it ends; L693, L595 and L808, slower by 19% to 46% beside unhindered PSUM readers, agree. **Rival 1** would have needed a DVE with room; the kernel with less DVE work shows it.

**Streaming: "on the path I put 0".** The blocks themselves come in time: TensorE waited 1.7 us for them in six periods. The price lies in the other transfers. The prediction named them ("A block load that waits for PE likewise holds the stage, v and swap transfers.") and gave them no term; rival 3 priced only the blocks' own lateness. The sinks' exchange (turns<-pt) takes 1.7 us from issue to landing in the six periods of the kernel before. In the changed kernel, and then without streaming in the last three pairs (KB, median us):

```profile
turns<-pt SPq DMA_DIRECT2D x6, 128.0 KB, 4.0
```
```profile
turns<-pt SPq DMA_DIRECT2D x6, 128.0 KB, 1.7
```

It stands in the chunk's last chain. From the one to the other, TensorE's wait for the sinks falls from 10.0 to 2.5 us in six periods and DVE's for the copies of x from 21.3 to 5.4. The other late transfers don't go with the cost: comb<-swap takes 4.7 and 4.6 us in the two, and v, 2.5 before, takes 3.6 in the products alone, which stream nothing. Whether the exchange is late by the queue's order or by the load on the DMA engines stays open: from ScalarE's queue the stream was no faster, but there the loads stand in ScalarE's order. A part is the clock's: 1.00 without streaming at the end, 0.98 with it, at most 0.02 x 59.1 = 1.2 us a period (an estimate).

**Making the weights: +2, bounds 0 and 8; measured 27.7 in chunks 0 to 2.** The 2.7 of chunk 3 are hardly its price: the products alone, which make no weights, take 55.01 us there too. I placed the work beside chunks 2 and 3, where the code stands. Nothing in the code holds GpSimd back until then, and the order of time on GpSimd has the first sum in chunk 0:

```profile
28.74 1.31 POOL L998 TENSOR_TENSOR exact<-w 128x512 f32<-128x512 f32 x1 [4.52 <-DVE w L435]
```

There DVE has no free time: of 40 us in chunks 0 and 1, first before, then after,

```profile
80.00:120.00 40.00, 39.73 (x262) 35.98 (x261) 38.90 (x84) 33.00 (x70) 1.67 (x3) 1.00 0.39 138
```
```profile
80.00:120.00 40.00, 35.13 (x219) 29.75 (x217) 39.86 (x52) 27.82 (x50) 16.30 (x13) 1.00 0.43 149
```

DVE did 52 instructions in place of 84 while busy throughout, and PE lost 4.6 us. GpSimd's 64 us were also 78: its three groups in chunks 0 to 2 average 937 (256 columns), 1568 and 1445 ns (512), not 730 and 1282. Holding it back moved the cost to chunk 4. How the 27.7 divide between the port and a plan that was ordered differently was not taken apart.

**Single score bank: 0.** Two banks gave the changed kernel a period of 57.3 instead of 59.1, and the products alone 53.2 instead of 52.2. With one run each and a new order in each, it stays open whether the bank costs time.

**The end: +1.0, bounds 0 and 3; measured 5.75 net, 8.5 with PE's gain.** The last instructions in order of time:

```profile
743.03 0.28 PE L1042 MATMUL bank<-xl,cut 128*128 128x256 f32 x1
743.35 0.59 ACT L1051 COPY both<-bank 128x512 f32<-128x512 f32 x1 [2.68 <-PE bank L1042]
743.97 0.43 DVE L1052 TENSOR_TENSOR both<-both 128x256 f32<-128x256 f32 x1 [2.71 <-ACT both L1051]
744.48 0.69 DVE L1053 TENSOR_TENSOR both<-bank,both 128x512 f32<-128x512 f32 x1
745.21 0.42 DVE L1055 TENSOR_TENSOR both<-bank,both 128x256 f32<-128x256 f32 x1
745.55 0.68 DVE L1056 TENSOR_TENSOR both<-bank,both 128x512 f32<-128x512 f32 x1
746.15 0.42 DVE L1057 TENSOR_TENSOR both<-bank,both 128x256 f32<-128x256 f32 x1
```

I counted two DVE operations behind ACT's copy; all five stand there in a row. From the last matmul's end to the end of the span it is 752.8 - 743.31 = 9.5 us; before it was 676.2 - 670.6 = 5.6. The last two output transfers, issued from ACT, took 4.5 us from issue to landing instead of 2.4 (medians of two). The other 1.9 of the 5.75 lie in chunk 11's stretch ahead of it.
